# State products in the same TensorE stretch as y, the first norm moved towards VectorE, new planner charges and places

## The chip, the cores and the metric

One core of a Trainium2 chip runs the whole program in one launch. The metric is the device time of one execution in microseconds; of three executions of the kernel before the median is 1108.64 us (1107.11 to 1110.08). PE is TensorE, DVE is VectorE, ACT is ScalarE, POOL is GpSimd, SP is the engine that only issues DMAs here.

## The reference

Three stages, all float32, on 4 batches of 768 tokens with 8 heads of 48 (3072 tokens of 384 in all):

```python
# 1. a linear recurrence with a complex diagonal decay, per batch and head
mag = sqrt(a_re**2 + a_im**2); scale = minimum(mag, 0.999) / (mag + 1e-6)
ar, ai = a_re * scale, a_im * scale
for t in range(S):
    S_re, S_im = ar*S_re - ai*S_im + outer(k[t], v[t]), ar*S_im + ai*S_re
    y[t] = q[t] @ S_re
# 2. x = relu(x @ w_in)**2 @ w_out                     (384 -> 2048 -> 384)
# 3. xn = x / sqrt(mean(x*x) + 1e-6) * rms_g
#    out = (silu(xn @ w_gate) * (xn @ w_val)) @ w_out  (384 -> 1536 -> 384)
```

## The kernel before, in words

The recurrence is cut into 24 **units**: chunk c (128 tokens, 6 chunks) of batch b, `u = 4*c + b`. Units are worked in sets: 0 and 1 alone, then in pairs (`SETS`). For each set a `chain` runs, mostly on DVE: `norm` (lines 346 to 377) turns the raw decay into the clipped one, seven `step`s multiply it up inside groups of eight tokens, `tot` transposes the group totals on PE, `plevel` scans them, `back` transposes them back, four products and two sums apply them, and `inv` divides k by the running product. Then for each unit: `prod` makes the packed tiles KP and QP (DVE), `turned` sends KP to DRAM and brings it back as `kt` with tokens on the partitions (two DMAs, kb and kt, on SP's queue, one buffer of kt), `dtr` transposes KP and QP on PE (tile dps, copied out by ACT), `score` multiplies them in two halves (sps, masked on DVE), `yy` makes y from the masked scores and V and, from the second chunk on, from the state and Q (yps, lines 590 and 594, copied out by ACT at line 598), and `state` makes 16 small products of kt and V (ups, line 640: 64 or 48 rows of output each, on two halves of the array; the profile counts 32 matmuls) and lets DVE add them to the state and decay it. Units 0 and 1 have their own y (`yy_direct`). Units 20 to 23 need no new state.

All of dps, sps, yps and ups come from one PSUM tag, `att`, with two buffers. A further buffer (`tb`) serves tot and back.

The layers of stage 2 run on groups of units (2, 2, 2, 2, 4, 4, 4, 4): 16 times `mlp_h` (9 matmuls, line 984) and `mlp_x` (9 matmuls, line 1010). Weights arrive as 64-bit words; `convert` cuts each of them into a high and a low part (ACT lines 672, 911, 920; DVE lines 674, 923; PE lines 917, 918). Stage 3 (`mlp_g`, `mlp_v`, line 1182, `mlp_o`, line 1010) starts near 655 us, after all units are done. These four kinds are called dense work below. The first of it starts at 70.05 us; until then PE also runs matmuls nobody reads (line 1320, tile `warm`) in its free time.

The order of the instructions on every engine is written out by a planner, `Plan.run`. Each `Op` carries an engine, a charge in us, buffers it takes and gives back, and names it waits for. Each job has a place: `PRI[kind]`, plus its position in the sweep, plus a shift from the table `SHIFT`, by the job's number in its kind. The planner walks through time with its charges and lets each engine take, of the jobs that are ready, the one with the lowest place; dense work on PE has 120 added, so that it runs when no other work is ready. The result is a fixed order per engine; on the chip each engine works through it in order, and waits only for data and buffers.

Lines of the kernel before that the change touches:

```python
yield Op("pe", 1.91 if c else 0.95, acq=["att"], rel=["st", "dq"], done=("y", u), p=soon(u))   # yy
yield Op("pe", 1.06, acq=["att"], rel=["kt"], done=("su", u))                                  # state
yield Op("none", 0, acq=["tmp", "tmp"])                                                        # inv
plan.job("state", max(q0, STATE0), att.state(u), [("kt", u), ("y", u)] + ...)
```

Of the kernel before, what the change touches and what calls it, by code (L numbers as in the profile page):

```python
# [9 lines left out]
F32 = mybir.dt.float32  # L10
# [36 lines left out]
SHIFT = dict(  # L47
    chain=((3, 6, -2),),
    convert=((4, 5, 1.5), (12, 15, -18.5),),
    decay=((5, 6, -37.5),),  # L50
    dtr_k=((7, 14, -21),),
    dtr_q=((2, 5, 76.5),),
    join=((41, 112, 72),),
    load_w2=((0, 9, -21.5),),
    load_x=((4, 6, 1),),
    mlp_h=((36, 39, -54.5),),
    mlp_o=((39, 72, 22.5),),
    mlp_x=((4, 96, -1.5), (96, 97, -33), (97, 125, -31.5),),
    prod_k=((14, 15, 2.5),),
    prod_q=((9, 11, 21), (18, 23, 12.5),),  # L60
    split=((0, 5, 43),),
    state=((6, 10, -8.5), (13, 20, 39),),
    store=((16, 18, 4),),
    store_x=((2, 11, -1),),
    turned=((4, 9, -31),),
)
LAND = 2.2
FILL, SWITCH = 18.0, 0.1
WINDOW, PHASE, RISE, STAY, SPARSE = 3.4133, 1.5, 0.45, 0.35, 0.45
# [6 lines left out]
OF = {u: (g, us.index(u)) for g, us in enumerate(GROUPS) for u in us}  # L76
DIRECT = (0, 1)
LAST = 3


# [4 lines left out]
def mm(k, n):  # L85
    return k * (0.006 + 0.0004375 * n)

# [21 lines left out]
class Plan:  # L109
# [25 lines left out]
    def ready(self, j):  # L135

        t, op = j[4], j[3]
        for n in (*j[5], *op.need):
            end, eng = self.t[n]
            t = max(t, end + after(eng, op.eng))  # L140
        for r in op.acq:
            k = self.taken[r] - self.counts[r]
# [79 lines left out]
class Attention:  # L222
# [11 lines left out]
    def __init__(self, ctx, tc, q, k, v, a_re, a_im, ident, sb, ps, dram):  # L234
# [17 lines left out]
        self.kin, self.qin, self.raw = {}, {}, {}  # L252
        self.kt, self.dt, self.st, self.Vg = {}, {}, {}, {}

# [36 lines left out]

    def tmp(self, name, dtype=F32):
        return self.sb.tile([128, 8 * 2 * D], dtype, tag="tmp", name=name, bufs=TMP)

# [8 lines left out]
    def load_a(self, g):  # L303
        if g == 0:
            yield Op("none", 3.8, acq=["raw", "raw"], done=("raw", 0))
        else:
            self.raw[g] = []
        for i in range(2):
            for c, src in enumerate((self.are, self.aim)):
                if g == 0 and i == 0:  # L310
                    continue
                u = 2 * g + i
                yield Op("sp", 0.65, acq=[] if i else ["raw"], mb=0.2, done=("raw", u) if c else None, free=True)
                if i == 0:
                    self.raw[g].append(self.sb.tile([128, 8 * 2 * D], F32, tag="raw", name="raw", bufs=2))
                self.nc.sync.dma_start(self.raw[g][c][:, i * 8 * D:(i + 1) * 8 * D], self.rows(src, u))
        yield Op("none", 0, done=("rawi", g))

# [27 lines left out]
    def norm(self, p):  # L346
# [11 lines left out]
        A = self.A[p % 2]  # L358
        m = self.tmp("m")[:, 0:w]
# [3 lines left out]
        yield from self.sumsq(m, y, raw, w)  # L363
        yield Op("act", act(w) + 0.2)
        nc.scalar.activation(out=r, in_=y, func=AF.Square, accum_out=self.ss[:, 0, p:p + 1])
        yield Op("dve", dve(w))
# [3 lines left out]
        yield Op("act", act(w))  # L370
        nc.scalar.activation(out=r, in_=y, func=AF.Copy, scale=-0.24975e-6, bias=-0.4995)
        yield Op("dve", dve(w))
# [68 lines left out]
    def chain(self, p):  # L441
# [49 lines left out]
    def inv(self, p):  # L491
# [4 lines left out]
        nc = self.nc  # L496
        yield Op("none", 0, acq=["tmp", "tmp"])
        n = len(SETS[p])
        w = n * 8 * D
        m, z = [self.tmp("m")[:, 0:w] for _ in range(2)]  # L500
        yield from self.sumsq(
# [10 lines left out]
        nc.vector.tensor_tensor(out=k, in0=k, in1=z, op=ALU.mult)  # L512
        yield Op("dve", dve(w), rel=["tmp", "tmp"], done=("inv", p))
        nc.vector.scalar_tensor_tensor(out=k, in0=m, scalar=2.0, in1=k, op0=ALU.subtract, op1=ALU.mult)
# [65 lines left out]
    def yy(self, u, xt):  # L580
        nc = self.nc
        b, c = self.bc(u)
        yield Op("pe", 1.91 if c else 0.95, acq=["att"], rel=["st", "dq"], done=("y", u), p=soon(u))
        V, St = self.V[u % 2], self.St[b]
        ST, Q = self.st.pop(u), self.dt["q", u]
        P = self.ps.tile([128, 4, CH], F32, tag="att", name="yps")
        for p in range(4):
# [3 lines left out]
            if c > 0:  # L591
                for z in range(2):
                    h = 2 * p + z
                    nc.tensor.matmul(  # L594
                        P[64 * z:64 * z + D, p], lhsT=St[:, h, :], rhs=Q[:, h, :], start=False, stop=True
                    )
        yield Op("act", act(512), rel=["att"], done=("xt", u))
        nc.scalar.mul(xt(), P, -1.0)

    def yy_direct(self, u, out):  # L600
        nc = self.nc
        yield Op("pe", 1.6, acq=["att"], rel=["xs", "gs"] if u == 1 else ["st", "dq", "xt"], done=("y", u), need=[("Vg", u)], p=soon(u))
        G, ST = self.Vg.pop(u), self.st.pop(u)
# [10 lines left out]
    def load_vg(self, u, pool):  # L614
# [15 lines left out]
        self.Vg[u] = G  # L630

    def state(self, u):
        nc = self.nc
        b, c = self.bc(u)
        yield Op("pe", 1.06, acq=["att"], rel=["kt"], done=("su", u))
        V, St, kt, pe = self.V[u % 2], self.St[b], self.kt.pop(u), self.pe[u % 4]
        P = self.ps.tile([112, H, D], F32, tag="att", name="ups")
        for h in range(H):
            for lo, hi in ((0, 64), (64, 112)):
                nc.tensor.matmul(P[lo:hi, h], lhsT=kt[:, h, lo:hi], rhs=V[:, h * D:(h + 1) * D], start=True, stop=True)  # L640
        re, im = pe[:, 0].unsqueeze(2), pe[:, 1].unsqueeze(2)
# [207 lines left out]
def kernel_body(ctx: ExitStack, tc, q, k, v, vt, a_re, a_im, w, rms_g, out):  # L849
# [185 lines left out]
    for g, us in enumerate(SETS):  # L1035
# [9 lines left out]
        for i, u in enumerate(us):  # L1045
# [21 lines left out]
            if att.more(u):  # L1067
                plan.job("turned", q0, att.turned(u), [("kP", u)] + ([("kt", u - 1)] if u else []))
                plan.job("state", max(q0, STATE0), att.state(u), [("kt", u), ("y", u)] + ([("su", u - 1)] if u else []))
# [298 lines left out]
```

## Time and profile before

| what | us |
|---|---|
| median of three executions | 1108.64 |
| the profiled execution, its own time | 1106.84 |
| its span in the profile | 1105.1 |
| PE busy | 1068.7 (97%) |
| DVE busy | 694.2 (63%) |
| ACT busy | 572.2 (52%) |

The span is the time from the first to the last instruction of the profiled execution; 1.7 us lie around it. Busy counts matmuls from their start to their modelled end, and in a run of matmuls they overlap. The distance from one group's start to the next one's start therefore says what the group costs PE; the timeline's rows below give it. Times in them count from the start of the span.

### The profile page before, as it was taken

The numbers are of one execution on the slowest core, as the hardware profiler recorded it, in microseconds if no ns is written. First come the engines' busy times: TensorE is split into PE (matmuls) and PEld (weight loads), VectorE is DVE, ScalarE is ACT, GpSimd is POOL, SyncE is SP. The second block draws the span as 40 slices with busy tenths as digits, with TensorE's granted clock in tenths as the row PEclk, the third lists the DMA queues.
The fourth block names the chain that finished last, engine by engine and source line by source line (L and its number), as shares of the span: only waits on it lengthen the run. The fifth ranks groups of instructions, "written<-read, shape, count | busy, mean of one in ns | idle before, by whom it ended". The sixth has DMA issues, their size and how long they took to land.

```text
span 1105.1 us, 17346 instructions
## 1 busy us (share of the span) xinstructions
PE 1068.7 (97%) x6806; PEld 913.0 (83%) x6806; DVE 694.2 (63%) x1414; ACT 572.2 (52%) x1123; POOL 4.0 (0%) x14
## 2 busy tenths in 40 slices
PE   3998989999999999999999999999999999999998
PEld 2887889999988888888888878888888888888886
DVE  7999999999999988877212876343251342431312
ACT  4788777676766655645445985241241331321212
POOL 1000000000000000000000000000000000000000
PEclk9999999999999999999999999999999999999999
DMA  9833334243344233211004641001010010000000
GB/s 326 278 98 99 81 98 131 79 116 98 108 115 109 56 107 96 59 41 60 10 3 185 226 163 58 29 29 29 1 58 1 4 54 1 1 29 1 29 0 32
DMA packets 80251, 85.53 MB, mean 77 GB/s; under 512 B 50528, under 2 KB 69792, under 8 KB 80160
## 3 DMA queue, kind: packets, MB, share of 16 engines
q1 hardware_dynamic: 79584, 83.61, 24.5%
q8 instruction: 55, 0.90, 0.4%
q10 hardware_dynamic: 576, 0.72, 0.2%
q14 instruction: 36, 0.29, 0.1%
HBM read 64.61 MB, written 18.61 MB: 75 GB/s over the span
## 4 chain that ended last, share of the span: by engine, by line
PE 73%; DVE 15%; ACT 4%; issue 2%; DMA 0%; DVEq 0%
PE v L1182 13%; PE g L1182 13%; PE o L1010 13%; PE h L984 12%; PE x L1010 12%; PE dps L556 2%; PE sps L573 2%; PE yps L590 1%; DVE XY L389 1%; PE yps L594 1%; PE ups L640 1%; DVE st L575 1%; DVE x L469 1%; ACT w L911 1%; DVE Y L652 1%
## 5 line engine op out<-in xcount | busy, mean ns | idle before, releaser
L1010 PE MATMUL x<-gs,w 128*128 128x256 f32 (+1 forms) x1152 | 228.9, 343 | 2.0 <-DVE gs L1004 0.9
L984 PE MATMUL h<-xs,w 128*128 128x256 f32 (+1 forms) x1152 | 224.6, 341 | 3.2 <-ACT gs L1001 2.4
L984 PEld LDWEIGHTS h<-xs,w 128*128 128x128 f32 x1152 | 178.9, 189 | 27.3 <-ACT gs L1001 3.3
L1010 PEld LDWEIGHTS x<-gs,w 128*128 128x128 f32 x1152 | 179.1, 189 | 27.0 <-DVE gs L1004 2.6
L1182 PE MATMUL g<-ys,w 128*128 128x512 f32 x648 | 158.6, 389 | 0.0
L1182 PE MATMUL v<-ys,w 128*128 128x512 f32 x648 | 158.5, 389 | 0.0
L1010 PE MATMUL o<-us,w 128*128 128x512 f32 x621 | 148.4, 389 | 0.0
L1182 PEld LDWEIGHTS g<-ys,w 128*128 128x128 f32 x648 | 121.6, 188 | 25.4
L1182 PEld LDWEIGHTS v<-ys,w 128*128 128x128 f32 x648 | 121.6, 188 | 25.3
L1010 PEld LDWEIGHTS o<-us,w 128*128 128x128 f32 x621 | 116.6, 188 | 24.2
L886 DVE TENSOR_TENSOR us<-uu,us 128x512 fp32r<-128x512 f32 x72 | 49.8, 692 | 135.8 <-ACT us L884 135.3
L1202 DVE TENSOR_TENSOR uu<-t,v 128x512 f32<-128x512 f32 x72 | 49.4, 687 | 123.4 <-PE v L1182 110.5
L991 ACT ACTIVATE r<-h 128x256 f32<-128x256 f32 (+1 forms) x128 | 62.4, 488 | 121.7 <-PE h L984 120.8
L1194 ACT ACTIVATE t<-g 128x512 f32<-128x512 f32 x72 | 43.0, 597 | 153.7 <-PE g L1182 137.4
L884 ACT CAST us<-uu 128x512 fp32r<-128x512 f32 x72 | 44.6, 620 | 142.5 <-DVE uu L1202 82.4
L1004 DVE TENSOR_TENSOR gs<-h,gs 128x512 fp32r<-128x512 f32 (+1 forms) x96 | 57.2, 598 | 46.0 <-ACT h L996 45.9
L994 ACT ACTIVATE gs<-r 128x256 fp32r<-128x256 f32 (+1 forms) x128 | 67.3, 527 | 5.2 <-PE x L1010 2.5
L996 ACT ACTIVATE h<-r 128x256 f32<-128x256 f32 (+1 forms) x128 | 62.3, 488 | 0.0
L389 DVE TENSOR_TENSOR XY<-A 128x384 f32<-128x384 f32 (+1 forms) x91 | 47.7, 524 | 1.6
L573 PEld LDWEIGHTS sps<-dq,dk 112*128 112x128 f32 x368 | 46.0, 191 | 3.2 <-ACT dq L558 0.9
L573 PE MATMUL sps<-dq,dk 112*128 112x128 f32 x368 | 48.0, 276 | 0.7 <-ACT dq L558 0.7
L672 ACT CAST top<-ws 128x384 f16<-128x384 bf16 x68 | 41.7, 628 | 0.6 <-DVE cr L674 0.5
(146 smaller groups left out, 1276.1 us busy)
## 6 DMA issues: line engine op xcount, KB each, us to landing
ws<-in_w SPq DMA_DIRECT2D x34, 767.8 KB, 6.9
kb<-KP SPq DMA_DIRECT2D x20, 448.0 KB, 5.2
kt<-kb SPq DMA_DIRECT2D x20, 448.0 KB, 4.3
raw<-in_a_re SPq DMA_DIRECT2D x24, 192.0 KB, 3.1
kin<-in_k SPq DMA_DIRECT2D x24, 192.0 KB, 3.6
qin<-in_q SPq DMA_DIRECT2D x24, 192.0 KB, 3.5
V<-in_vt SPq DMA_DIRECT2D x24, 192.0 KB, 4.2
xr<-xnd SPq DMA_DIRECT2D x6, 768.0 KB, 4.3
```

The lines of the kernel that those rows point to most:

```text
L389: nc.vector.tensor_tensor(out=T, in0=v.unsqueeze(1).to_broadcast([128, 2, 2, n]), in1=w.unsqueeze(2).to_broadcast([128, 2, 2, n]), op=ALU. ...
L573: nc.tensor.matmul(P[:, i], lhsT=K[:, h, :], rhs=Q[:, h, :], start=True, stop=True)
L884: nc.scalar.copy(out=hi, in_=src)
L886: nc.vector.tensor_tensor(out=lo, in0=src, in1=hi.bitcast(F32), op=ALU.subtract)
L984: nc.tensor.matmul(hp, lhsT=part(f, 0, a)[:, kk * 128:(kk + 1) * 128], rhs=xs[:, bb, kk, :], start=(i == 0), stop=(i == 8),)
L991: nc.scalar.activation(out=r, in_=hp, func=AF.Relu)
L994: nc.scalar.activation(out=gs[:, 0], in_=r, func=AF.Square)
L996: nc.scalar.activation(out=hp, in_=r, func=AF.Square)
L1004: nc.vector.tensor_tensor(out=gs[:, 1], in0=hp, in1=gs[:, 0].bitcast(F32), op=ALU.subtract)
L1010: nc.tensor.matmul(ps[e], lhsT=w(bb)[:, e * 128:(e + 1) * 128], rhs=src[:, a, :], start=(first and n == 0), stop=(last and n == 2),)
L1182: nc.tensor.matmul(P, lhsT=part(T_GATE + f, half, a)[:, kk * 128:(kk + 1) * 128], rhs=ys[:, bb, kk, :], start=(i == 0), stop=(i == 8),)
L1202: nc.vector.tensor_tensor(out=uu, in0=t_t.pop((g, f)), in1=P, op=ALU.mult)
```

## The change

Four things. In `yy`, for every unit from 2 to 19, the 32 matmuls of `state` are issued directly behind those of y, in one planner operation that takes two `att` buffers, waits for `kt` of its unit too and gives `kt` back; `state` then holds only the DVE part. In `norm`, for set 0 alone, the second square, the square of the reciprocal root and the linear step run on DVE, not on ACT, and the accumulating square of ACT goes off into an unused half of the tile. In `inv`, sets from 3 on take two buffers of the tag `cr` (the one `convert` uses) and not two of `tmp`. And the planner's numbers change: charges of dense matmuls, of tiled matmuls and of the first loads, and nearly the whole table `SHIFT`, which had 28 entries and has some 260.

```diff
-    chain=((3, 6, -2),),
-    convert=((4, 5, 1.5), (12, 15, -18.5),),
...
+    chain=((0, 2, 1.5), (2, 3, 2), (3, 6, 1.5), (6, 8, 3.5), (8, 9, -11), (9, 10, 15.5), (10, 11, 8),
+        (11, 13, -8),),
+    convert=((0, 5, -14.5), (5, 6, -6.5), (6, 7, -14.5), (7, 10, -10.5), (10, 11, -9), (11, 12, -56.5),
+        (12, 13, -9), (13, 14, -8.5), (14, 16, -10.5),),
...
+    prod_k=((0, 19, -3), (19, 20, -1.5), (20, 24, -3),),
+    prod_q=((0, 1, -10.5), (1, 5, 16), (5, 9, 33.5), (9, 10, 32), (10, 12, 33.5), (12, 14, 15.5), (14, 17, 84),
+        (17, 18, 15.5), (18, 21, 5), (21, 22, 29.5), (22, 24, 44),),
...
-FILL, SWITCH = 18.0, 0.1
+FILL, SWITCH, TILED = 18.0, 0.12, 0.09
+RAW1 = 2.6
...
+TAIL = 0.82
 LAST = 3
+FAST = (0,)
+SPARE = 3
...
 def mm(k, n):
-    return k * (0.006 + 0.0004375 * n)
+    return k * (n + 33) / 2400
...
-            yield Op("none", 3.8, acq=["raw", "raw"], done=("raw", 0))
+            yield Op("none", 4.55, acq=["raw", "raw"], done=("raw", 0))
...
+        fast = p in FAST
+        if fast:
+            yield Op("act", act(w))
+            nc.scalar.activation(out=m, in_=raw[0], func=AF.Square)
+            yield Op("dve", dve(w), free=True)
+            nc.vector.tensor_tensor(out=y, in0=raw[1], in1=raw[1], op=ALU.mult)
+            yield Op("dve", dve(w))
+            nc.vector.tensor_tensor(out=m, in0=m, in1=y, op=ALU.add)
+            yield Op("act", act(w))
+            nc.scalar.activation(out=y, in_=m, func=AF.Abs_reciprocal_sqrt, bias=self.tiny)
+            yield Op("dve", dve(w))
+            nc.vector.tensor_tensor(out=r, in0=y, in1=y, op=ALU.mult)
+            yield Op("act", act(w) + 0.2, free=True)
+            nc.scalar.activation(out=t[:, w:2 * w], in_=y, func=AF.Square, accum_out=self.ss[:, 0, p:p + 1])
+        else:
+            yield from self.sumsq(m, y, raw, w)
...
+        if fast:
+            yield Op("dve", dve(w // 2))
+            nc.vector.tensor_scalar(
+                out=r, in0=y, scalar1=-0.24975e-6, scalar2=-0.4995, op0=ALU.mult, op1=ALU.add
+            )
+        else:
+            yield Op("act", act(w))
+            nc.scalar.activation(out=r, in_=y, func=AF.Copy, scale=-0.24975e-6, bias=-0.4995)
...
-        yield Op("none", 0, acq=["tmp", "tmp"])
+        tag, bufs = ("cr", 2) if p >= SPARE else ("tmp", TMP)
+        yield Op("none", 0, acq=[tag])
+        yield Op("none", 0, acq=[tag])
...
-        yield Op("pe", 1.91 if c else 0.95, acq=["att"], rel=["st", "dq"], done=("y", u), p=soon(u))
+        both = self.joined(u)
+        yield Op(
+            "pe", (1.91 if c else 0.95) + TILED + (TAIL if both else 0.0), acq=["att", "att"] if both else ["att"],
+            rel=["st", "dq"] + ["kt"] * both, done=("y", u), p=soon(u),
+        )
...
+        if both:
+            self.products(u)
+        yield Op("none", 0, done=("su", u) if both else None)
...
+    def joined(self, u):
+        return u not in DIRECT and self.more(u)
+
+    def products(self, u):
+        V, kt = self.V[u % 2], self.kt.pop(u)
+        P = self.up[u] = self.ps.tile([112, H, D], F32, tag="att", name="ups")
         for h in range(H):
             for lo, hi in ((0, 64), (64, 112)):
-                nc.tensor.matmul(P[lo:hi, h], lhsT=kt[:, h, lo:hi], rhs=V[:, h * D:(h + 1) * D], start=True, stop=True)
+                self.nc.tensor.matmul(
+                    P[lo:hi, h], lhsT=kt[:, h, lo:hi], rhs=V[:, h * D:(h + 1) * D], start=True, stop=True
+                )
+
+    def state(self, u):
...
+        if not self.joined(u):
+            yield Op("pe", 1.06 + TILED, acq=["att"], rel=["kt"], done=("su", u))
+            self.products(u)
+        P, St, pe = self.up.pop(u), self.St[b], self.pe[u % 4]
...
-                + ([("y", u - 1)] if u else []),
+                + ([("y", u - 1)] if u else []) + ([("kt", u), ("su", u - 1)] if att.joined(u) else []),
```

## Rows read from the trace of the kernel before

**Rows 1.** The page: the span.
```profile
span 1105.1 us, 17346 instructions
```

**Rows 2.** Windows: us, then busy us (count) of PE, PEld, DVE, ACT, POOL, clock, DMA.
```profile
70.00:150.00 80.00, 69.82 (x634) 62.17 (x633) 77.26 (x172) 64.16 (x157) 0.00 (x0) 1.00 0.29 78
150.00:320.00 170.00, 168.48 (x1709) 160.48 (x1709) 161.15 (x365) 121.50 (x296) 0.00 (x0) 1.00 0.41 112
320.00:520.00 200.00, 200.00 (x1445) 166.89 (x1440) 174.55 (x355) 121.26 (x230) 0.00 (x0) 1.00 0.27 77
```

**Rows 3.** What PE waited for from 70 to 150 us: total, times, longest.
```profile
PE dps L556 <- DVE KP L523: 2.7, 2, 2.3
PE dps L556 <- DVE QP L523: 1.5, 1, 1.5
```

**Rows 4.** PE's timeline (start us, us, instructions): plain dense work, y alone, products alone.
```profile
77.57 1.25 PE L984 MATMUL h<-xs,w 128*128 128x256 f32 x9
78.65 1.24 PE L1010 MATMUL x<-gs,w 128*128 128x256 f32 x9
...
157.92 0.39 PE L594 MATMUL yps<-dq,St 112*48 112x128 f32 x4
158.24 1.34 PE L1010 MATMUL x<-gs,w 128*128 128x256 f32 x9
159.42 0.60 PE L556 MATMUL dps<-ident,KP 128*112 128x128 f32 x4
...
161.04 1.24 PE L1010 MATMUL x<-gs,w 128*128 128x256 f32 x9
162.21 1.13 PE L640 MATMUL ups<-V,kt 128*64 128x48 f32 x32
163.27 0.65 PE L556 MATMUL dps<-ident,QP 128*112 128x128 f32 x4
...
497.61 1.13 PE L640 MATMUL ups<-V,kt 128*64 128x48 f32 x32
```

**Rows 5.** The same view: products right behind y.
```profile
217.31 0.39 PE L594 MATMUL yps<-dq,St 112*48 112x128 f32 x4
217.53 1.08 PE L640 MATMUL ups<-V,kt 128*64 128x48 f32 x32
218.54 2.42 PE L984 MATMUL h<-xs,w 128*128 128x256 f32 x18
```

**Rows 6.** Timeline of ACT and DVE, 4 to 10 us: steps of the first norm.
```profile
4.88 0.51 ACT L340 ACTIVATE A<-raw 128x384 f32<-128x384 f32 x1
5.49 0.56 DVE L342 TENSOR_TENSOR m<-m,A 128x384 f32<-128x384 f32 x1 [2.92 <-ACT A L340]
6.29 0.52 ACT L340 ACTIVATE m<-raw 128x384 f32<-128x384 f32 x1 [0.90 <-DMA raw<-in_a_re]
6.71 0.60 ACT L344 ACTIVATE A<-m,tiny 128x384 f32<-128x384 f32 x1
7.99 0.56 DVE L367 TENSOR_TENSOR m<-m,A 128x384 f32<-128x384 f32 x1 [1.95 <-ACT A L365]
8.66 0.56 DVE L369 SCALAR_TENSOR_TENSOR A<-m,A 128x384 f32<-128x384 f32 x1
9.88 0.56 DVE L373 SCALAR_TENSOR_TENSOR m<-A 128x384 f32<-128x384 f32 x1 [0.19 <-ACT A L371]
```

**Rows 7.** Groups by line: DVE's tensor-scalar form on 512 columns.
```profile
L1168 DVE TENSOR_SCALAR rs_t<-rs_t 128x512 f32<-128x512 f32 x6 | 2.6, 427 | 0.2
```

**Rows 8.** PE's timeline: unit 2's y, and its products.
```profile
106.58 1.09 PE L590 MATMUL yps<-st,V 128*64 128x128 f32 x16
...
111.87 1.13 PE L640 MATMUL ups<-V,kt 128*64 128x48 f32 x32
```

**Rows 9.** Around rows 5: the window (columns as rows 2), and DVE's addition of the products.
```profile
215.00:222.00 7.00, 7.00 (x100) 6.81 (x99) 6.92 (x12) 3.63 (x10) 0.00 (x0) 1.00 0.15 30
218.94 0.55 DVE L648 TENSOR_TENSOR St<-ups,St 112x384 f32<-112x384 f32 x1
```

More of the change, by code (lines that the diff above doesn't have):

```diff
@@ L47 @@
 SHIFT = dict(
-    chain=((3, 6, -2),),
-    convert=((4, 5, 1.5), (12, 15, -18.5),),
[L50 to L62, printed above, removed]
@@ new lines @@
+    decay=((1, 2, -8), (2, 3, -5), (3, 4, -8), (4, 5, -36), (10, 13, -23.5),),
+    dtr_k=((0, 1, -1), (1, 2, -4), (2, 3, 10.5), (3, 11, -4), (11, 22, -1), (22, 24, 4),),
+    dtr_q=((0, 2, -5.5), (2, 7, -1.5), (7, 9, -54), (9, 10, -53), (10, 12, -54), (12, 19, -56), (19, 20, -54.5),
+        (20, 22, -2), (22, 23, -9), (23, 24, -13),),
+    fix=((7, 8, -25.5), (14, 18, 3.5), (18, 19, -2), (19, 22, 3.5),),
+    join=((0, 14, -1), (14, 17, -13), (17, 27, -1), (27, 29, 1), (29, 50, -1), (50, 51, 5), (51, 62, -1),
+        (62, 63, 3.5), (63, 75, -2), (75, 96, 3.5), (96, 108, 69), (108, 114, 133),),
@@ new lines @@
+    rms=((0, 1, -1.5), (1, 2, 3.5), (2, 3, 10), (3, 4, 13.5), (4, 6, 11),),
+    score=((0, 3, -6), (3, 4, 17.5), (4, 43, -6), (43, 44, -5.5), (44, 48, -6),),
+    split=((0, 4, 23), (4, 6, 30), (6, 8, 25), (8, 9, 28), (9, 14, 26), (14, 15, 20.5), (15, 22, 26),),
+    state=((0, 1, -5), (1, 2, -1), (2, 5, -5), (5, 6, 18.5), (6, 7, -5), (7, 9, 1), (9, 10, 1.5), (10, 11, 1),
+        (11, 15, 1.5), (15, 17, 16.5), (17, 20, 46.5),),
+    store=((0, 4, -8), (4, 5, -2), (5, 6, -4.5), (6, 10, -8), (10, 12, -9.5), (12, 14, -38.5), (14, 15, -64),
+        (15, 16, -68.5), (16, 17, -69), (17, 18, -36.5), (18, 19, -43.5),),
@@ L140, in ready @@
             t = max(t, end + after(eng, op.eng))
-        for r in op.acq:
-            k = self.taken[r] - self.counts[r]
+        for i, r in enumerate(op.acq):
+            k = self.taken[r] + op.acq[:i].count(r) - self.counts[r]
             if k >= 0:
@@ L312, in load_a @@
                 u = 2 * g + i
-                yield Op("sp", 0.65, acq=[] if i else ["raw"], mb=0.2, done=("raw", u) if c else None, free=True)
+                yield Op("sp", 0.65, acq=[] if i else ["raw"], mb=0.2, done=("raw", u) if c and g else None, free=True)
                 if i == 0:
@@ L316, in load_a @@
                 self.nc.sync.dma_start(self.raw[g][c][:, i * 8 * D:(i + 1) * 8 * D], self.rows(src, u))
+        if g == 0:
+            yield Op("none", RAW1, done=("raw", 1))
         yield Op("none", 0, done=("rawi", g))
@@ L358, in norm @@
         A = self.A[p % 2]
-        m = self.tmp("m")[:, 0:w]
+        t = self.tmp("m")
+        m = t[:, 0:w]
         y, r = [A[:, c].rearrange("p j x -> p (j x)")[:, 0:w] for c in range(2)]
@@ L362, in norm @@
         raw = [t[:, u % 2 * 8 * D:u % 2 * 8 * D + w] for t in self.raw[u // 2]]
[L363 to L366, printed above, removed]
+        fast = p in FAST
[14 more added lines that the diff above has]
+            yield from self.sumsq(m, y, raw, w)
+            yield Op("act", act(w) + 0.2)
+            nc.scalar.activation(out=r, in_=y, func=AF.Square, accum_out=self.ss[:, 0, p:p + 1])
+        yield Op("dve", dve(w), free=fast)
         nc.vector.tensor_tensor(out=m, in0=m, in1=r, op=ALU.mult)
@@ L457, in chain @@
             )
-        yield Op("none", 0, acq=["tmp", "tmp"])
+        yield Op("none", 0, acq=["tmp"])
+        yield Op("none", 0, acq=["tmp"])
         k = len(SETS[p])
@@ L496, in inv @@
         nc = self.nc
-        yield Op("none", 0, acq=["tmp", "tmp"])
+        tag, bufs = ("cr", 2) if p >= SPARE else ("tmp", TMP)
+        yield Op("none", 0, acq=[tag])
+        yield Op("none", 0, acq=[tag])
         n = len(SETS[p])
         w = n * 8 * D
-        m, z = [self.tmp("m")[:, 0:w] for _ in range(2)]
+        m, z = [self.tmp("m", I32 if p >= SPARE else F32, tag, bufs).bitcast(F32)[:, 0:w] for _ in range(2)]
         yield from self.sumsq(
@@ L601, in yy_direct @@
         nc = self.nc
-        yield Op("pe", 1.6, acq=["att"], rel=["xs", "gs"] if u == 1 else ["st", "dq", "xt"], done=("y", u), need=[("Vg", u)], p=soon(u))
+        yield Op("pe", 1.6 + TILED, acq=["att"], rel=["xs", "gs"] if u == 1 else ["st", "dq", "xt"], done=("y", u), need=[("Vg", u)], p=soon(u))
         G, ST = self.Vg.pop(u), self.st.pop(u)
@@ L630, in load_vg @@
         self.Vg[u] = G
+    def joined(self, u):
[3 more added lines that the diff above has]
+        P = self.up[u] = self.ps.tile([112, H, D], F32, tag="att", name="ups")
+        for h in range(H):
+            for lo, hi in ((0, 64), (64, 112)):
+                self.nc.tensor.matmul(
+                    P[lo:hi, h], lhsT=kt[:, h, lo:hi], rhs=V[:, h * D:(h + 1) * D], start=True, stop=True
+                )
     def state(self, u):
@@ L1068, in kernel_body @@
                 plan.job("turned", q0, att.turned(u), [("kP", u)] + ([("kt", u - 1)] if u else []))
-                plan.job("state", max(q0, STATE0), att.state(u), [("kt", u), ("y", u)] + ([("su", u - 1)] if u else []))
+                plan.job("state", max(q0, STATE0), att.state(u), [("kt", u), ("y", u)] + ([("su", u - 1)] if u and not att.joined(u) else []))
                 plan.job("join", q0, join([("y", u), ("su", u)], ["V"]))
```

40 lines of the change are left out of this document (26 added, 14 removed).

## The prediction

> **What bounds the kernel now.** I read the stage windows first, then PE's waits, then PE's timeline, and last the timeline of the first 12 us. The windows [rows 2] are to be read by PE's first number against the length: from 320 to 520 us PE is busy for all 200.00 us, from 150 to 320 for 168.48 of 170. There the time is PE's work, and only fewer or shorter stretches of PE help. The clock column says 1.00 in every stage, the upper of the two levels (2.4 GHz), so no clock explains any of it. From 70 to 150 us PE stands still for 80 - 69.82 = 10.2 us while DVE is busy for 77.26 of 80: here DVE bounds, and PE waits for what it makes [rows 3]. Before 70 us nothing dense runs; what starts it is the chain of sets 0 and 1, which begins with the first norm. So there are three places to gain: PE's own work after 150 us, the 10.2 us before it, and an earlier start of the chain on DVE.
>
> The profiled execution took 1106.84 us, its span 1105.1 [rows 1]; the median of three is 1108.64, 1.8 us more. I work out differences against the profiled one and put them on the median.
>
> **The change part by part.** *Products behind y.* The trace holds the old arrangement and, twice by chance, the new one. What a group costs is read from its start to the next one's start. Dense work among its like takes 78.65 - 77.57 = 1.08 us; the same nine matmuls ahead of the products 162.21 - 161.04 = 1.17, so running into the small forms costs 0.09. Nine dense matmuls behind the small forms and ahead of a transposition take 159.42 - 158.24 = 1.18, so coming out costs 0.10. The products alone take 163.27 - 162.21 = 1.06, and y's last four matmuls 158.24 - 157.92 = 0.32 [all rows 4]. Where products follow y, these two last 218.54 - 217.53 = 1.01 and 217.53 - 217.31 = 0.22 [rows 5]. A join therefore saves 0.05 + 0.10 = 0.15 us always, 0.09 or 0.10 more on each side where dense work stood, 0.34 at most. Units 4 to 19 come after 150 us; two of these 16 are joined already, so 14 stretches go, the first at 162 us, the last at 498 [rows 4]. Most have a transposition on one side; I take 0.20 each, near the case with one dense neighbour (0.24) and short of it because some have attention work ahead. 14 x 0.20 = 2.8. Units 2 and 3 add 2 x 0.34 = 0.7, if PE matters there. Sum 3.5; ends 14 x 0.15 = 2.1 and 16 x 0.34 = 5.4. The V and kt that the products read are not copied again and no instruction is added; the DVE part of `state` stays.
>
> The join adds waits. A y now needs kt, and the DMAs kb and kt ahead of it. Unit 2's y began at 106.58, its products, held until kt was there, at 111.87 [rows 8]: 5.3 us would be the price if nothing else moved. Behind the waiting y on PE stand all later groups, dense ones too, and behind it in data xt, its DMAs, the split and the first dense work of units 2 and 3. But the table of places puts the products with k ahead (all `prod_k` by 3) and those with q back (`prod_q` of units 1 to 11 by 16 to 33), so KP, and with it kb and kt, should leave DVE earlier against QP. I take nothing for it, and keep 5.3 us as the far end. For the later units the old spacing of y leaves kt room, so it is not summed. SP's queue is in order too, and kt may sit behind the small xt DMAs; the same far end covers that.
>
> A joined y also needs both `att` buffers at once. I take zero, since both score halves must have been masked before y can start, so both were free a moment before; the price if a transposition has taken one in between is a rival below.
>
> *First norm.* The path now [rows 6]: the second square starts at 4.88 on ACT, the sum at 5.49 on DVE, but the root at 6.71, because ACT had stepped into a square of set 1 at 6.29 that waited 0.90 us for its data. Then the products at 7.99 and 8.66, and the clip at 9.88. With the change, a square on DVE at 4.88 and the 0.67 us from one dependent DVE instruction to the next (8.66 - 7.99) put the sum at 5.55 and its end at 6.11. The wait for set 1 is planned later (its data has its own landing charge), so the root starts at about 6.2, ends at 6.8; the square of it on DVE 6.9, products 7.57 and 8.24, the linear step 8.91. That form took 0.427 us on 512 columns [rows 7], about 0.34 on 384, so with 0.11 us between the clip comes at about 9.36: 0.52 us earlier. If the imaginary part lands sooner than ACT could show, the square starts up to 0.4 us sooner. I take 0.7, ends 0 and 0.9. The added DVE work, two squares and the linear step, is 0.56 + 0.56 + 0.34 = 1.5 us; it lies in waits of 2.92 and 1.95 us [rows 6]. Were these filled, it would cost up to 1.5 us on a DVE that bounds until 150 us; that is the end below nothing. What is late next is the chain itself, in step on DVE up to the first dense work.
>
> *Buffers of the inverse.* From set 3 on it takes `cr` and not `tmp`. Cost 0, gain 0: after 150 us DVE waits do not end the path, and before it only set 3 is touched; at the far end one pair of weight cuts waits for it, which is inside the 5.3 above.
>
> *Places and charges.* They reorder everything; the diff does not give the new order, so I bound it. A gain can't exceed the standing time of PE that an order can mend: 10.2 us from 70 to 150 and 1.5 from 150 to 320 [rows 2], 11.7. A loss is bounded by the same kind of wait: the 5.3 us above. The row nearest to what an order mends is PE's wait for KP (2.7) and QP (1.5) [rows 3]: there a transposition stood at the head of PE's queue before its operand was made, and dense work could have gone first. I take these 4.2 us.
>
> Sum: 3.5 + 0.7 + 4.2 = 8.4 us. The profiled 1106.84 becomes 1098.4, the median about 1100.2.
>
> **The rivals.** (A) *The gaps close.* Joins at their upper end, 5.4, the norm 0.9, all 11.7 us of standing: 18.0, about 1091. For it: dense work exists from 70 us on, and the waits of [rows 3] are of 2.3 us at most. Against: DVE has 2.7 us left from 70 to 150, so less than half can come from filling it.
>
> (B) *The places bring nothing.* What is left is 3.5 + 0.7 = 4.2: 1104.4. For it: DVE's 97% in that stage, whatever the order.
>
> (C) *kt is late.* PE stands for unit 2 as long as its products did: 8.4 - 5.3 = 3.1 gained, 1105.5. For it: rows 8. Against: the table moves k ahead of q.
>
> (D) *The second buffer: slower.* A joined y holds both buffers until ACT has copied y and DVE has added the products. In the one joined case the products ended at 218.54 and their addition at 218.94 + 0.55 = 219.49 [rows 5, 9]: 0.95 us in which no transposition or score can begin, and in which PE needs dense work ready. If each of 18 joined units costs PE these 0.95 us, 17.1 us come on top: 1108.64 - 8.4 + 17.1 = 1117.3. It eats the gain from 8.4 / 18 = 0.47 us a unit and makes the kernel measurably slower from 0.65. For it: two buffers, and DVE late from 70 to 320. Against: in that same joined case PE was busy for 7.00 of 7 us [rows 9], as dense work stood behind it. The Trainium skill bears on this, "TensorEngine Tiling (Array Packing)", section Performance Considerations: tiling speeds up TensorE but not the evacuation of PSUM, which may then bound. By that rule this rival would hold; the trace, with its 7.00 of 7, does not show it, though one window at 217 us says little of the stage before 150.
>
> **How the numbers follow.** Forecast, 1096 to 1103.5: 0.45. A 0.16, B 0.14, C 0.13, D 0.12. A change under about 0.3%, 3.3 us, cannot be told from none here: same is 1105.3 to 1112.0. Faster takes the forecast, A, 0.11 of B and 0.02 of C: 0.74. Same: 0.03 of B and 0.11 of C, 0.14. Slower: D, 0.12. The range goes from A's 1091 to 1109, beyond C, and leaves out D and the outer half of A.
>
> **What would show it.** Right: no group of products between other work from unit 2 on, 1.01 us each; PE idle from 70 to 150 at about 6 us and no wait for KP over 1 us; the clip of the first norm near 9.4 and the first dense matmul a little before 70 us. Wrong: PE waits at y whose releaser is a kt DMA (C) or the copies of yps and ups, or waits of dps and sps for the addition (D); DVE still full with the same idle of PE (B). The forecast is wrong as a whole if the stretch after 320 us, which hardly depends on order, starts later against its work than now.

## The result, and the profile after

The changed kernel takes 1114.31 us (median of five runs, 1113.26 to 1115.79); beside it the kernel before took 1108.64 (1107.11 to 1110.88). The ratio is 1.0054, 95% interval 1.0043 to 1.0065: slower by 5.7 us, where 8.4 us of gain were forecast. The profiled execution grew by 6.5 us of span [rows 1]:

```profile
span 1111.6 us, 17412 instructions
```

The windows of the changed kernel (columns as in rows 2):

```profile
70.00:150.00 80.00, 70.46 (x620) 64.09 (x620) 73.94 (x159) 67.13 (x161) 0.00 (x0) 0.96 0.27 76
150.00:320.00 170.00, 163.20 (x1674) 157.01 (x1672) 159.02 (x353) 117.83 (x290) 0.00 (x0) 1.00 0.38 104
320.00:520.00 200.00, 198.25 (x1453) 166.25 (x1453) 178.53 (x376) 121.75 (x232) 0.00 (x0) 1.00 0.30 82
```

Set against [rows 2], PE stands still for 9.54 us in the first stage (10.18 before), for 6.80 in the second (1.52 before) and for 1.75 in the third (0 before). In all that is 18.1 us where there were 11.7. The first stage has become a little better; the loss is in the middle stage, which had been nearly full. DVE is busy for less there, 159.02 us against 161.15, and in the first stage 73.94 against 77.26. So PE does not stand because DVE has more to do; DVE stands too.

The joined stretch is there for every unit from 2 to 19, right behind y (`yps` is y's output, `ups` that of the products). The PE timeline of unit 4:

```profile
168.71 0.39 PE L654 MATMUL yps<-dq,St 112*48 112x128 f32 x4
168.93 1.08 PE L703 MATMUL ups<-V,kt 128*64 128x48 f32 x32
169.94 0.41 PE L508 MATMUL back<-ident,TP 112*128 112x112 f32 x2
```

y's last four matmuls take 0.22 us and the products 1.01, as in [rows 5]; no group of ups stands alone from unit 2 on. From start to next start, all groups of yps and ups together take 61.7 us where they took 64.3: in these groups the join saves 2.6 us of PE's work. What it saves on the dense groups beside them is not in that number.

The first norm, DVE's timeline:

```profile
4.00 0.56 DVE L400 TENSOR_TENSOR A<-raw 128x384 f32<-128x384 f32 x1 [1.43 <-DMA raw<-in_a_im]
...
7.84 0.56 DVE L416 SCALAR_TENSOR_TENSOR A<-m,A 128x384 f32<-128x384 f32 x1 [0.20 <-ACT m L408]
...
8.83 0.56 DVE L426 SCALAR_TENSOR_TENSOR m<-A 128x384 f32<-128x384 f32 x1
```

The clip stands at 8.83, 1.05 us earlier than in [rows 6]. But the first dense work starts later, at 71.51 us (70.05 before); what holds it back is not taken apart:

```profile
71.51 2.41 PE L1057 MATMUL h<-xs,w 128*128 128x256 f32 x18
```

What PE waits for in the first stage, and then in the second (total, times, longest):

```profile
PE dps L612 <- DVE QP L579: 2.1, 2, 1.8
PE h L1057 <- ACT w L993: 1.9, 2, 1.2
PE h L1057 <- ACT gs L1074: 1.6, 2, 1.1
```

```profile
PE x L1083 <- DVE gs L1077: 1.8, 2, 1.3
PE x L1083 <- ACT gs L1074: 1.3, 3, 0.7
PE dps L612 <- ACT dq L614: 1.2, 3, 0.7
PE dps L612 <- DVE KP L579: 0.9, 1, 0.9
```

In the first stage the wait for KP of [rows 3] is gone (0.9 us is left, after 150 us). The wait for QP stays (2.1 us, 1.5 in [rows 3]), waits for cut weights (w) are 1.9 us (0.5 before), and the dense work's own step (gs, made by ACT or DVE between h and x) holds PE as it did before. In the second stage PE had waited for gs for 0.3 us in all; now it is 3.1. No y waits for kt, and the waits for the DVE step that reads the products and frees their buffer are 0.7 us between 70 and 520 us. Waits for any holder of the two `att` buffers (copies, masks, products) are 3.0 us there, 0.8 before. After some waits PE runs at the lower of its two levels, 1.2 GHz:

```profile
145.29 1.07 PE L612 MATMUL dps<-ident,QP 128*112 128x128 f32 x4 [1.82 <-DVE QP L579]
146.01 2.27 PE L1083 MATMUL x<-gs,w 128*128 128x256 f32 x9
```

Nine matmuls that take 1.24 us [rows 4] take 2.27 here, behind a stand of 1.82; the clock column reads 0.96 for the stage. It is one of two such stretches; the other begins at 76.99 us, behind stands of 0.99 and 1.14.

At the end of the second stage PE runs out of dense work:

```profile
312.61 1.08 PE L703 MATMUL ups<-V,kt 128*64 128x48 f32 x32
313.62 1.34 PE L1083 MATMUL x<-gs,w 128*128 128x256 f32 x9
314.79 0.60 PE L612 MATMUL dps<-ident,QP 128*112 128x128 f32 x4
315.23 0.60 PE L612 MATMUL dps<-ident,KP 128*112 128x128 f32 x4
316.07 0.65 PE L612 MATMUL dps<-ident,QP 128*112 128x128 f32 x4 [0.24 <-ACT dq L614]
316.56 0.65 PE L612 MATMUL dps<-ident,KP 128*112 128x128 f32 x4
317.88 2.05 PE L629 MATMUL sps<-dq,dk 112*128 112x128 f32 x16 [0.68 <-ACT dk L614]
321.03 1.41 PE L612 MATMUL dps<-ident,KP 128*112 128x128 f32 x8 [1.10 <-DVE st L631]
322.37 0.65 PE L459 MATMUL tot<-ident,A 128*48 128x128 f32 x8
322.96 4.38 PE L1057 MATMUL h<-xs,w 128*128 128x512 f32 x18
```

From 314.8 to 323.0 there is only attention work with gaps of 0.24, 0.68 and 1.10 us. The next dense work, on groups of four units (128x512), needs units 8 to 11. y of unit 8 had begun at 254.4 us (250.5 before), of unit 11 at 310.8 (303.3 before). That dense work started at 314.3 us before and starts at 323.0 now; from there on each dense matmul comes 6 to 12 us later than the same one before, at the end 6.5.

Taken over PE's stretch from its first dense matmul to its last matmul, before and after:

```profile
70.05:1100.42 1030.37, 1017.71 (x6449) 869.15 (x6447) 632.12 (x1229) 528.54 (x1034) 0.00 (x0) 1.00 0.21 64
```

```profile
71.51:1106.89 1035.38, 1017.03 (x6417) 871.62 (x6413) 633.82 (x1228) 532.87 (x1041) 0.00 (x0) 1.00 0.22 64
```

So the 6.5 us are 1.5 of later start and 5.7 of standing (18.4 us for 12.7; up to 520 us it is 6.4 more, behind that 0.7 less), less 0.7 of PE's work. The join's 2.6 us are in that 0.7, and most of them are lost again in other groups; the lower clock is one reason, the rest is not taken apart.

### The profile page after: what moved, and what is told of

The parts are those of the page before. It is cut to its first block, busy times and chain, and to the rows that moved or that the text cites. A ratio compares the mean times of both kernels' runs of the same rounds, so it can differ in the third digit from the quotient of the medians.

```text
span 1111.6 us, 17412 instructions
## 1 busy us (share of the span) xinstructions
PE 1070.9 (96%) x6825; PEld 917.9 (83%) x6825; DVE 696.7 (63%) x1417; ACT 572.1 (51%) x1121; POOL 4.0 (0%) x14
## 4 chain that ended last, share of the span: by engine, by line
PE 67%; DVE 6%; ACT 2%; issue 1%; DVEq 0%; ACTq 0%
PE v L1255 13%; PE g L1255 13%; PE o L1083 13%; PE x L1083 10%; PE h L1057 10%; PE dps L612 2%; PE sps L629 2%; PE yps L650 1%; PE yps L654 1%; DVE gs L1077 1%; PE ups L703 1%; DVE XY L442 0%; ACT top L745 0%; PE o L1303 0%; ACT w L984 0%
```

## The experiments

O is the theory that the joined stretch costs what it was priced at and the order loses; D is the prediction's rival of the second buffer. In the first four the order is kept and one part is undone or done alone. Ratios are to the kernel before, timed beside each run.

**new_apart**: the changed order, the products issued behind the group that follows y.

```diff
         if both:
-            self.products(u)
+            self.late = u
...
+    def flush(self):
+        u, self.late = self.late, None
+        if u is not None:
+            self.products(u)
```

`flush` is called behind each dense group and ahead of each attention group.

> The changed kernel with every instruction of DVE, ACT and SP in the same order, and on PE the products of units 2 to 19 issued behind the next other group instead of right behind y (18 moves, 16 of them behind dense work). Theory O (the loss comes from the new order; the join itself saves 0.24 to 0.34 us a unit): slower than the changed kernel's 1114.3 us by 18 x 0.24 to 0.34 = 4.3 to 6.1 us, about 1119.5. Rival D (two buffers held at once, or the wait for kt, cost up to 0.95 us a unit): not slower, 1114 or below.

1128.92 us (1127.49 to 1129.34), ratio 1.0188 (1.0174 to 1.0203). D falls by its own sign: taking the joined stretches apart gives nothing back, it costs 14.6 us. It is also 9 us above O. The same stretch as above, from the first dense matmul to PE's last:

```profile
74.70:1122.25 1047.55, 1025.45 (x6417) 870.62 (x6413) 633.92 (x1228) 532.86 (x1041) 0.00 (x0) 1.00 0.21 63
```

Against the changed kernel 3.2 us are from the start, where ACT stood 3.56 us at a weight cast whose DMA was late (the last section); PE stands 3.8 us longer (22.1 for 18.4); and 8.4 us are PE's work, where O had 4.3 to 6.1. As far as one run tells, products between other groups cost PE more than I had priced, and an order stretched at 18 places adds waits.

**old_join6**: the order before, with the products of units 3, 5, 6, 8, 9 and 13 moved behind their y.

```diff
+        if u in (3, 5, 6, 8, 9, 13):
+            self.products(u)
```

> The kernel before with its order kept, and in six units (3, 5, 6, 8, 9, 13) the products moved up right behind y. Theory O: faster than before's 1108.6 us by 6 x 0.24 to 0.34 = 1.4 to 2.0 us, about 1106.9. Rival D: slower by up to 6 x 0.95 = 5.7 us, up to 1114.

1108.8 us (1108.12 to 1112.2) where the kernel before had 1107.79: ratio 1.0013 (1.0004 to 1.0022). Neither theory. PE's work fell by 1.2 us, 0.21 a join, as priced; yet the windows and PE's waits from 150 to 320 us show

```profile
150.00:320.00 170.00, 166.31 (x1689) 159.47 (x1688) 159.58 (x362) 120.39 (x294) 0.00 (x0) 1.00 0.41 112
```

```profile
PE h L993 <- DVE gs L1013: 1.2, 2, 0.9
PE x L1019 <- DVE gs L1013: 1.0, 2, 0.6
```

3.69 us of standing for 1.52 [rows 2], now for gs. I read it so: the separate products had been cover for the step from h over ACT and DVE to x, and with them gone PE reaches the dense work sooner and waits there. The four waits stand behind joins (at 207.4 and 214.4 us behind unit 6's, at 263.0 and 274.3 behind those of units 8 and 9); no run puts other work in the products' place, so this stays argued.

**new_slow_norm**: the changed order, three steps of the norm back on ACT.

```diff
-            nc.vector.tensor_tensor(out=y, in0=raw[1], in1=raw[1], op=ALU.mult)
+            nc.scalar.activation(out=y, in_=raw[1], func=AF.Square)
...
-            nc.vector.tensor_tensor(out=r, in0=y, in1=y, op=ALU.mult)
...
-            nc.scalar.activation(out=t[:, w:2 * w], in_=y, func=AF.Square, accum_out=self.ss[:, 0, p:p + 1])
+            nc.scalar.activation(out=r, in_=y, func=AF.Square, accum_out=self.ss[:, 0, p:p + 1])
...
-            nc.vector.tensor_scalar(
-                out=r, in0=y, scalar1=-0.24975e-6, scalar2=-0.4995, op0=ALU.mult, op1=ALU.add
-            )
+            nc.scalar.activation(out=r, in_=y, func=AF.Copy, scale=-0.24975e-6, bias=-0.4995)
```

> The changed kernel in its own order with the first norm's second square, square of the root and linear step back on ACT. Theory O: the first norm gives 0.5 to 0.9 us to the start of the chain, and what is left of it at the end is between 0 and that: 1114.3 to 1115.2. If the first norm on DVE costs time on a full DVE: up to 1.5 us faster, 1112.8.

1115.71 us (1113.62 to 1116.9), ratio 1.0073 (1.006 to 1.0086). Its interval overlaps that of the changed kernel; the first dense work moved to 72.73 us. By the ratios the norm is worth about 2 us in this order, if anything, and is not the loss.

**new_filled**: 30 matmuls that nobody reads in the two gaps ahead of half-clock stretches.

```diff
+            if (u, which, half) == (4, "q", 0):
+                for j in range(14):
+                    nc.tensor.transpose(P[:, j % 4], self.ident[:, 0:112], self.ident)
...
+        if (g, f) == (0, 1):
+            for _ in range(16):
+                plan.fill()
```

> The changed kernel with matmuls that nobody reads put into PE's two long gaps before its half-clock stretches (16 behind the second dense group, 14 transpositions ahead of unit 4's first one), 30 in all. Rival K (the loss is the clock: about 3 us lost at half clock): granted clock 1.00 from 70 to 150 us and about 3 us less, 1111.3. Theory O: the clock comes back too, but DVE bounds there, so the end moves by 1.5 us at most, 1112.8 to 1114.5.

1113.7 us (1112.24 to 1114.56), ratio 1.0054 (1.0042 to 1.0067), the ratio of the changed kernel itself; that is O's window, above K's 1111.3. The profiled span is 1.1 us shorter (1110.5), and the clock column of the first stage is back at 1.00:

```profile
70.00:150.00 80.00, 72.37 (x659) 65.71 (x660) 74.95 (x162) 68.39 (x164) 0.00 (x0) 1.00 0.28 75
```

The standing in the second stage stays (150 to 320 us: 163.13 busy). But of the two stretches at the lower level only one is gone: one begins at 149.71 us now, behind a stand of 1.68, and so falls outside the window. The run prices one stretch, at 0 to 1.1 us. That the clock (K) is not the loss is seen better in new_slack below: its first stage reads 0.96 too, and it is the fastest of all.

In the next ones the order itself is the question. All but old_places replace the planner's choice by a list:

```diff
-        while live:
...
+        for i in range(0, len(ORDER), 2):
+            n = DIGITS.index(ORDER[i]) * 64 + DIGITS.index(ORDER[i + 1]) - 1
...
+            j = self.jobs[n]
...
```

`ORDER` names the job of each next operation, with two characters for each; every operation of every job comes once. The list starts as the old or the changed order. Single operations were moved, and a move was kept where the end by the planner's charges came sooner (the joined products charged at 0.98 us, near the 1.01 of the trace).

**new_reordered**: all instructions of the changed kernel, another order.

> The changed kernel with every one of its instructions (joined products, VectorE norm, spare buffers), emitted in another order: single operations of the first 560 us were moved in the plan's own price list until its end came earlier (joined products charged at 0.98 us, near the 1.01 us of the trace, in place of 0.82: 1089.0 us where the changed order has 1108.7). O (the order that the new places give is the loss, and the join is not): well below the kernel before, 1095 to 1105 us, TensorE's idle time after 70 us cut from 18 us to 12 or less. J (the joined stretch itself costs, by its later y and its two buffers): it stays at 1110 to 1115 us in any order, since all 18 joined stretches are in it.

1103.21 us (1100.82 to 1104.7), ratio 0.9951 (0.994 to 0.9963): 11 us below the changed kernel with the same instructions, and below the kernel before. PE's standing from 70 to 520 us is 11.6 us. O holds, J falls.

**old_reordered**: the instructions of the kernel before, moved in the same way.

> The kernel before with its own instructions (products apart, norm mostly on ScalarE), order moved in the same way in the first 560 us (1088.9 us in the plan's prices where the old order has 1100.6). O: 1095 to 1105 us, as far below the kernel before as new_reordered within 3 us, so that the join is worth 0 to 3.5 us once the order fits it. J: clearly faster than new_reordered, by 6 us or more.

1102.9 us (1102.29 to 1103.08), ratio 0.9951 (0.9938 to 0.9964), the same as new_reordered. So most of what was to be had lay in the order, and join and norm together cannot be told from nothing here. "Apart" is not quite true of this kernel: in its order five of the 18 units have their products right behind y (two in the kernel before).

**old_norm**: the order before, written as a list, and the changed `norm`, three steps of it on DVE.

```diff
+FAST = (0,)
...
+            nc.vector.tensor_tensor(out=y, in0=raw[1], in1=raw[1], op=ALU.mult)
...
+            nc.vector.tensor_tensor(out=r, in0=y, in1=y, op=ALU.mult)
...
+            nc.vector.tensor_scalar(
+                out=r, in0=y, scalar1=-0.24975e-6, scalar2=-0.4995, op0=ALU.mult, op1=ALU.add
+            )
```

> The kernel before, its order kept, with the first norm's square, product and linear step on VectorE as in the changed kernel: the norm alone. If the norm's saving reaches the end as my sum had it: 0.7 us below the kernel before (1107.9 where that reads 1108.6). If the later weight cuts eat it, because VectorE's early work and not the norm's length sets the first dense work: no difference, -0.3 to +1.5 us.

1107.72 us (1106.77 to 1109.46), ratio 1.0000 (0.9991 to 1.0009): nothing, although an interval of 1 us either way would hardly show the 0.7 that was hoped for. The clip comes 0.57 us earlier (9.31), the first dense work 0.5 later:

```profile
70.58 2.59 PE L1071 MATMUL h<-xs,w 128*128 128x256 f32 x18
```

DVE is busy for 62.51 of its first 70 us there, where the chain of sets 0 and 1 and the weight cuts share it; that 1.5 us more on it eat what the shorter norm gives fits both times, and is argued from them. A rival fits as well: ACT reaches the cast of the first weights sooner, waits 2.48 us for their DMA and starts it at 10.22 (9.76 before, without a wait), 0.46 us later. No run tells the two apart.

**old_places**: the changed kernel with the old table of places.

```diff
-    chain=((0, 2, 1.5), (2, 3, 2), (3, 6, 1.5), (6, 8, 3.5), (8, 9, -11), (9, 10, 15.5), (10, 11, 8),
-        (11, 13, -8),),
...
+    chain=((3, 6, -2),),
...
```

> The changed kernel with the table of places of the kernel before: join, norm, spare buffers and new charges without the new places. My sum had the three other parts at a gain of 4 us or more without the places. O: the old table does not fit the new work at all (by the plan's own prices its end is 29 us later than with the new table): 1125 to 1145 us. Parts that can be added up: 1104 to 1112 us.

1136.62 us (1134.66 to 1137.37), ratio 1.0253 (1.024 to 1.0266). Here the windows show PE standing in every stage:

```profile
70.00:150.00 80.00, 70.57 (x614) 61.86 (x613) 76.69 (x162) 67.39 (x158) 0.00 (x0) 0.96 0.28 77
150.00:320.00 170.00, 161.75 (x1610) 155.01 (x1609) 154.11 (x341) 115.91 (x289) 0.00 (x0) 1.00 0.37 98
320.00:520.00 200.00, 192.12 (x1393) 159.45 (x1392) 171.53 (x367) 117.95 (x222) 0.00 (x0) 0.99 0.31 83
```

A table fits one set of charges and operations. Its parts do not add up: join, norm, buffers and charges without the new places lose 28.6 us, so no part's worth can be read by undoing it in the planner.

**new_mid** and **new_early**: the changed order, moved only between 120 and 340 us, or only before 120 us.

> The changed kernel's instructions and its order outside 120 to 340 us; inside, single operations moved (14.9 us in the plan's prices; new_reordered's 19.7 us there were 11.1 us on the chip). M (the loss lies in the order between 120 and 340 us, where state and split work that nobody waits for stands ahead of what attention waits for on VectorE): 1104 to 1108 us, below the kernel before, TensorE's idle time of 150 to 400 us from 8.3 us to 3 or less. E (the loss comes from before 120 us: late start, half clock, weight cuts not done; the later stage inherits it): 1111 us or more.

> The changed kernel's order beyond 120 us; before that, single operations moved (2.5 us in the plan's prices). M: 1111.5 to 1114.5 us, at most 2 us below the changed kernel. E: 1109 us or less.

new_mid: 1108.67 us (1106.3 to 1110.79), ratio 1.0005 (0.9996 to 1.0014), 0.7 us above the window of M and 2.3 below E's. new_early: 1112.89 (1112.33 to 1113.19), ratio 1.0045 (1.0032 to 1.0058), in M's window. Half of what the whole reordering gives lies between 120 and 340 us, an eighth before; the rest needs both, or the stage behind. PE's standing from 150 to 400 us falls from 8.6 to 3.3 (M said 3 or less), from 150 to 320 us from 6.80 to 2.57:

```profile
150.00:320.00 170.00, 167.43 (x1702) 160.72 (x1702) 165.81 (x366) 122.02 (x301) 0.00 (x0) 1.00 0.39 106
```

Some of what was moved is seen on DVE. First the changed kernel, then new_mid; Y and St are the decay of unit 3's state, which nobody reads until unit 7's y (a first chunk has no older state to add to):

```profile
129.03 1.12 DVE L725 TENSOR_TENSOR Y<-ups,pe 48x384 f32<-48x384 f32 x2
130.17 0.56 DVE L729 TENSOR_TENSOR St<-ups,pe 112x384 f32<-112x384 f32 x1
...
131.11 0.55 DVE L731 TENSOR_TENSOR St<-St,Y 112x384 f32<-112x384 f32 x1
...
160.79 0.69 DVE L631 TENSOR_TENSOR st<-sps,mask 128x512 f32<-128x512 f32 x1 [2.41 <-PE sps L629]
```

```profile
148.30 0.55 DVE L764 TENSOR_TENSOR Y<-ups,pe 48x384 f32<-48x384 f32 x1
...
149.16 0.56 DVE L764 TENSOR_TENSOR Y<-ups,pe 48x384 f32<-48x384 f32 x1
149.73 0.56 DVE L768 TENSOR_TENSOR St<-ups,pe 112x384 f32<-112x384 f32 x1
...
162.63 0.55 DVE L770 TENSOR_TENSOR St<-St,Y 112x384 f32<-112x384 f32 x1
```

In the changed kernel 2.2 us of it stand at 129 to 131.7, ahead of other work; later DVE reaches the mask of unit 4's scores before PE has made them and stands for 2.41 us. In new_mid the same operations stand at 148 to 163, and the longest wait of DVE from 150 to 320 us is 0.6. From unit 2's y it takes 52.0 us to unit 4's (54.6 in the changed kernel) and 188.7 to unit 11's (198.3). Counted from the start of the span the two profiles don't compare: new_mid's first stage ran 3 us later in the same order, for a reason given at the end. The Trainium skill, "PSUM — Partial Sum Buffer", section Engine vs sequencer instructions, says that VectorE's queue is a strict FIFO; the 2.41 us agree. These rows are an example: new_mid moves many operations, and none was moved alone.

The same rows speak against D. The products of unit 3 in new_mid,

```profile
129.31 1.08 PE L742 MATMUL ups<-V,kt 128*64 128x48 f32 x32
```

end at 130.39 and are last read at 149.73 + 0.56 = 150.29: they hold one of the two `att` buffers for 20 us, where D priced 0.95 for both. PE shows no wait for that buffer; the one group that needs one meanwhile, at 146.47, waits for its operand QP.

**new_slack** and **old_slack**: as new_reordered and old_reordered, but the order is moved for the mean end of four lists of charges, three of them with operations of DVE, ACT and POOL up to 22 per cent longer.

> All instructions of the changed kernel as in new_reordered, the order of the first 560 us moved for the mean end of four price lists, in three of which each operation of VectorE, ScalarE and GpSimd is up to 22 per cent longer (1088.2 us in the list without that, 1089.0 for new_reordered). If new_reordered lost 8.4 us between its plan and the chip because its order leaves no slack for operations that come late: 1096 to 1101 us, the fastest of all. If that loss is of prices alone: 1102 to 1104 us.

> The kernel before's instructions (products apart, norm mostly on ScalarE), order moved as for new_slack (1089.5 us in the list without longer operations). Slack: 1096 to 1101 us, and against new_slack the join and norm at one and the same treatment: within 2 us of it if they are worth nothing once the order fits (new_reordered against old_reordered: 0.3 us), 3.5 us above new_slack if they are worth what my sum gave the join.

new_slack: 1096.99 us (1096.8 to 1098.65), ratio 0.9902 (0.9888 to 0.9916), the fastest of all: 10.9 us below the kernel before, 17.3 below the changed one, whose instructions it has. old_slack: 1098.19 us (1097.82 to 1098.89), ratio 0.9915 (0.9902 to 0.9928). Join and norm are worth 1.2 us between them, with overlapping intervals; each order was searched for by itself, and old_slack's too has five of the 18 products right behind y. The windows of new_slack:

```profile
70.00:150.00 80.00, 72.99 (x613) 66.63 (x614) 76.33 (x162) 69.32 (x167) 0.00 (x0) 0.96 0.29 83
150.00:320.00 170.00, 168.41 (x1754) 162.42 (x1753) 164.66 (x376) 123.63 (x298) 0.00 (x0) 1.00 0.42 112
320.00:520.00 200.00, 200.00 (x1423) 169.69 (x1421) 168.13 (x349) 118.55 (x226) 0.00 (x0) 1.00 0.29 79
```

PE stands for 7.01, 1.59 and 0 us: 8.6 in place of 18.1. That is not the whole gain. From the first dense matmul to PE's last:

```profile
69.86:1092.26 1022.40, 1013.49 (x6417) 872.37 (x6413) 632.67 (x1230) 532.65 (x1041) 0.00 (x0) 1.00 0.22 66
```

PE ends 14.6 us sooner than in the changed kernel: 1.7 by the earlier start, 9.5 by less standing, and 3.5 because its work, with the same matmuls, is shorter (1013.5 for 1017.0). For old_slack against the kernel before it is 4.1 (1013.6 for 1017.7) of 8.9. The order sets PE's work too, by how often PE passes between dense and other groups: by the traces, from the first dense matmul on, 263 times before and 245 in the changed kernel, 215 in new_slack and 207 in old_slack. At the prediction's 0.09 to 0.10 us a change, 30 changes make an estimated 2.9 us, 56 make 5.3.

## Why the prediction was wrong

**The step that failed is *Places and charges*.** It took 4.2 us of gain from PE's waits for KP and QP, with 11.7 of gain and 5.3 of loss as ends. Measured, PE's standing did not fall by 4.2 us but rose by 6.4 up to 520 us (11.7 to 18.1), beyond the lower end. Set beside the profile, the three terms of the sum read: start of the dense work, 0.7 sooner forecast, 1.5 later measured; standing, 4.2 less forecast, 5.7 more measured over the whole; PE's work, 3.5 less forecast, 0.7 less measured. The bounds of the failed term had been read from rows of the old order: the standing that an order could mend, and one wait that it could make. But an order is not confined to the waits that the old one has. It made new ones in the stage that I had called PE-bound, 150 to 320 us, where [rows 2] show 168.48 of 170 busy. I took that stage as PE's work and free of order; it was full, as the runs show, because its order was good. new_reordered and new_slack show the step by itself: the same instructions, 11 and 17 us faster than the changed kernel by order alone. The upper end was wrong in kind too: an order can also shorten PE's work, as new_slack and old_slack show.

**Products behind y**: the size per group was right (0.22 and 1.01 us, 0.21 saved in old_join6; 2.6 us measured in the groups of y and products, of 3.5 forecast with the dense neighbours), its arrival at the end was not. At one order (old_join6) it turned into waits, mostly for gs, and lost 1.4 us by the ratio; with the order made anew, join and norm together are worth 1.2 us or nothing. "If PE matters there" should have been asked for every unit: work is worth its time only if what stands behind it is ready.

**First norm**: the clip came earlier than forecast (8.83 against 9.36, 1.05 us sooner where 0.9 was the end), but the first dense work did not: it came later in the changed kernel and in old_norm (1.0000). That an earlier clip starts the dense work earlier was a premise without a row. The 1.5 us added to DVE were costed at nothing because they lie in waits of [rows 6]; that they cost it behind 9 us, the end that I gave as "below nothing", is argued, not shown.

**Buffers of the inverse**: no step of an inverse waits for a buffer in the trace after; not tried alone.

**The signs that I named**: PE's standing from 70 to 150 us was to be 6 us; it is 9.54. KP's wait went, as forecast; QP's, which I had also counted as gained, stayed at 2.1 us. The first dense matmul came later. The sign for "wrong as a whole" was that the stretch after 320 us starts later against its work, and so it does: 323.0 against 314.3.

**The rivals.** D gave the right side and nearly the size (1117.3), by a mechanism that isn't there. That the number is near is luck. The waits for the step that frees the products' buffer are 0.7 us, new_mid holds such a buffer for 20 us without a wait for it, and new_slack with all 18 joins is the fastest. The rule that I weighed with it, of the Trainium skill's "TensorEngine Tiling (Array Packing)", section Performance Considerations (evacuation may bind where tiling is faster), was not what bound here. C falls: no y waits for kt. Unit 2's y did begin 5.9 us later (112.46 for 106.58), close to C's 5.3, but its kt had been asked for at 103.0 us, sooner than before (106.7), and PE worked on other groups. A and B are excluded by the time; B's thought, that places bring nothing, erred to the good side. I gave slower 0.12, all of it to D; the ordinary way to lose, an order that is a little worse in the fullest stage, had no chance of its own.

Not settled: which of the table's entries lose (it has 217, 23 before; the counts of 260 and 28 ahead of the prediction are wrong), since new_mid and new_early together recover 7.1 of the 17.3 us, and how much the charges did apart from the places.

## What to carry to other kernels

Where a planner writes the order and the change replaces its table, the table is the change: bound its effect by the whole standing that any stage could have, also in stages that are full now, and by what the changes between kinds of work cost, and give "a worse order" its own chance. Work taken off a busy engine gains only if its successor is ready, so look at what the removed work had covered. And an order made for exact charges is fragile: one made for charges with some slack was worth another 4 to 6 us on the chip, for both sets of instructions.

## What the runs showed that I had not expected

With exact charges the plan ended at 1089.0 us and TensorE's work on the chip at 1097.4 (new_reordered); with slack at 1088.2 and 1092.3 (new_slack). The distance halves without any change of the instructions. With the old instructions the plan's end even came later with slack (1089.5 for 1088.9), and the chip's time fell from 1102.9 to 1098.2.

And the changed order has made the first norm hang on a weight's DMA. ACT takes a cast of the first weights ahead of the norm's accumulating square, and DVE's next step overwrites what that square reads. In the changed kernel's profile the weights had landed (the cast starts at 6.71 us, after 0.25 of waiting). In new_mid, in the same order up to 120 us, they had not; ACT's timeline and DVE's:

```profile
9.89 0.62 ACT L784 CAST top<-ws 128x384 f16<-128x384 bf16 x1 [3.42 <-DMA ws<-in_w]
10.38 0.51 ACT L447 ACTIVATE m<-A 128x384 f32<-128x384 f32 x1
```

```profile
7.10 0.56 DVE L453 TENSOR_TENSOR m<-m,A 128x384 f32<-128x384 f32 x1
11.02 0.56 DVE L455 SCALAR_TENSOR_TENSOR A<-m,A 128x384 f32<-128x384 f32 x1 [3.36 <-ACT m L447]
```

Step and clip come 3.18 us later than in the changed kernel (11.02 for 7.84), and the first dense work at 74.69 us for 71.51. new_apart had the same (3.56 us of waiting), new_filled and new_slow_norm not (0.34 and 0.27). In the kernel before the cast stands behind the norm's work, at 9.76, and does not wait. So the earlier clip is also the less certain one. It was lost in two of these five profiles with the changed early order, too few to say how often.
